# Channel sums by matmuls of 512 columns over four rows at a time, in three shifted banks, in place of one matmul of 384 columns for each row

## The chip, the cores and the metric

The kernel runs on one core of one Trainium2 chip. The metric is the device time of one execution in microseconds (us). The span in a profile starts and ends a little inside the measured time (532.4 us of span for a profiled run of 534.2 us), so spans are compared with spans and times with times.

## The reference

The input x is 384 x 384 pixels of 384 channels in bf16. Every channel is averaged over all pixels, the mean is scaled by one weight and passed through a sigmoid, and x is multiplied by that gate.

```python
g = jnp.einsum("bhwc->bc", x) / (H * W)      # H = W = C = 384, B = 1
s = gp[:, 0:C] * w1d[0]                      # k = 1: no padding, one tap
s = _sigmoid(s)
return x * s[:, None, None, :]
```

One property of these inputs matters for what the runs can prove. The weight is 0.00123 and no channel's mean is above 0.001 in size, so all 384 gates round to 0.5 in bf16. The output would be right with badly wrong sums, so "correct" says here that the data arrived and was multiplied, and does not prove the sums right.

## The kernel before

x is 147,456 rows of 384 channels: 1152 groups of 128 rows, one row for each partition. A "row" below is one such group: 384 elements, 768 bytes, on each of 128 partitions. Tiles of 45 and 44 rows are loaded into an arena that holds six of them. The first three tiles give an early gate; every tile is multiplied by that early gate and stored at once. The sums go on to the last tile only to check at the end that the early gate equals the true one in bf16. If it didn't, the whole pass would be run again.

```python
TILE = 45
AHEAD_TILES = 3
...
def add_rows(place, n, bank, first, last):          # TensorE: a sum over partitions and rows
    for i in range(n):
        plan.op("tensor",
            lambda e, i=i: e.matmul(acc[bank][:, :C], ones[:], at(place + i, 1),
                                    start=first and i == 0, stop=last and i == n - 1), ...)

def put(place, n, r0):                              # VectorE: the gate; ScalarE's queue: the store
    plan.op("vector", gate(place, n, s_early), reads=["s_early"] + rows(place, n), ...)
    plan.final.append(plan.dma("scalar", dram(o_rows, r0, n), at(place, n), ...))

for k, n in enumerate(sizes):
    place = ring.take(n)                            # an arena place: its old tile must be stored
    while inside and any(...): put(*inside.pop(0))
    load(place, n, r0)                              # SyncE's queue
    ...
    add_rows(place, n, 0 if k < AHEAD_TILES else 1, ...)     # condensed from two calls
    if k == AHEAD_TILES - 1:
        # VectorE: total <- acc[0]; ScalarE: s_early <- sigmoid(total * scale)
        ...
# after the last tile: total += acc[1], s_true, compare with s_early
```

The order of work for a tile is thus: load, sums (TensorE), gate (VectorE, which waits for the sums to have read the tile), store, and only then may a new load use the place.

## Time and profile before

| | before |
|---|---|
| time, median of the first 3 runs | 533.75 us (533.66 to 533.89) |
| bytes read and written | 113.25 + 113.25 MB |
| DMA rate in the steady state | 433 GB/s |
| TensorE busy | 243.2 us, 46% |
| VectorE busy | 236.7 us, 44% |
| blocks of instructions fetched | 9 |

First, lines from the page of the profile of the kernel before. The page's strips cut the span into 40 equal slices: the digits are tenths of busy time of TensorE (PE), VectorE (DVE) and the DMA engines, the next line is what they moved (a packet is counted whole in the slice where it starts, so single slices swing about the mean). "q8" is the queue that brings instructions: packets, MB, share of the DMA engines' time. The last two are groups of instructions: operation, shapes, count, then busy us and mean ns of one, then the idle time before them and what ended it.

```profile
...
PE   0979643347156156266266156266265255165100
...
DVE  0006999551642642633633642632633642633700
...
DMA  9999999999999999999999999999999999999995
GB/s 371 418 450 421 411 415 454 418 449 417 447 416 449 414 448 425 434 442 423 432 444 424 432 443 421 434 444 415 439 444 421 434 440 424 434 442 423 432 440 241
...
q8 instruction: 9, 0.15, 0.1%
...
L206 PE MATMUL acc<-arena,ones 128*128 128x384 bf16 x1152 | 243.0, 383 | 249.2 <-DMA arena<-in_x_dram 249.2
L165 DVE TENSOR_TENSOR arena<-arena,s_early 128x16896 bf16<-128x16896 bf16 (+1 forms) x26 | 234.1, 9019 | 224.3 <-PE acc L206 223.6
...
```

The DMA strip is full from the first slice to the last but one, while TensorE and VectorE are idle about half the time. Read this as: the DMA engines are the bound, and a busy or idle TensorE is a question for the waits. Next the windows view of the same kernel: for each stretch of time its length, the busy us of each engine with counts, TensorE's granted clock, the DMA's share and its rate in GB/s (by where a packet starts).

```profile
...
core 0: us, PE busy (x) PEld busy (x) DVE busy (x) ACT busy (x) POOL busy (x), PEclk, DMA share, GB/s
...
115.00:135.00 20.00, 9.72 (x45) 5.08 (x45) 8.67 (x2) 0.00 (x0) 0.00 (x0) 0.74 1.00 433
515.00:525.00 10.00, 0.00 (x0) 0.00 (x0) 0.00 (x0) 0.00 (x0) 0.00 (x0) 0.50 1.00 433
...
527.00:528.00 1.00, 0.00 (x0) 0.00 (x0) 0.00 (x0) 0.00 (x0) 0.00 (x0) 0.50 0.16 68
529.00:530.00 1.00, 0.00 (x0) 0.00 (x0) 0.00 (x0) 0.00 (x0) 0.00 (x0) 0.50 0.08 34
530.00:532.40 2.40, 0.00 (x0) 0.00 (x0) 0.00 (x0) 0.00 (x0) 0.00 (x0) 0.50 0.00 0
...
```

The rate is 433 GB/s both in the middle and ten microseconds before the end, when only stores are left. The Trainium skill ("DMA: Bandwidth & Descriptors", Specifications) gives 435 GB/s as the fabric ceiling for one core, and this trace agrees over long windows (single slices of the strip read up to 454, by the way in which packets are counted). Two short stretches will matter later: 68 GB/s at 527 to 528 us and 34 GB/s at 529 to 530 us.

The list of waits (engine, line and releaser: us in total, times, longest) and, after it, that of the queue which issues the loads:

```profile
...
PE acc L206 <- DMA arena<-in_x_dram: 249.2, 26, 18.0
DVE arena L165 <- PE acc L206: 223.6, 20, 11.9
...
```

```profile
...
SPq L99 <- DMA out_dram<-arena: 444.6, 20, 74.5
...
```

TensorE waits for loads, VectorE for TensorE, and the issue of loads waits for stores to free arena places. The waits for loads and stores are long while the DMA engines are full. That VectorE waits for TensorE doesn't show that a faster TensorE would help.

Finally the start, from the timeline of the same kernel (start, length, engine, line, operation): the sums of the third tile, the copy of the sums, the sigmoid, the first two gates and the issue of the first store.

```profile
...
35.46 9.07 PE L206 MATMUL acc<-arena,ones 128*128 128x384 bf16 x45 [3.95 <-DMA arena<-in_x_dram]
...
44.57 0.56 DVE L249 COPY total<-acc 128x384 f32<-128x384 f32 x1 [42.10 <-PE acc L206]
45.16 0.62 ACT L255 ACTIVATE s_early<-total,w_scaled 128x384 bf16<-128x384 f32 x1 [42.38 <-DVE total L249]
...
45.81 18.23 DVE L165 TENSOR_TENSOR arena<-arena,s_early 128x17280 bf16<-128x17280 bf16 x2 [0.68 <-ACT s_early L255]
55.00 0.38 ACTq L91 DMA_DIRECT2D out_dram<-arena  x1
...
```

The first store is issued at 55.00 us. Nothing can be stored before it, but six loads are in the queue and keep the DMA engines busy past 60 us.

### The profile page before, as it was taken

How to read it: one execution, taken by the hardware profiler on the slowest of the kernel's cores; microseconds unless marked ns; L12 is line 12 of the kernel's file. 1: busy time of each engine (PE TensorE's matmuls, PEld its weight loads, DVE VectorE, ACT ScalarE, POOL GpSimd, SP SyncE). 2: the span in 40 equal slices, each digit the busy share in tenths (PEclk: the TensorE clock that was granted, in tenths of full speed). 3: DMA queues.
4: the chain of work that ended last, by engine and by line, in shares of the span. 5: the costliest groups of instructions: out<-in, count | busy, mean ns of one | idle time of the engine just before them, and what ended most of it. 6: DMA issues, size and time to landing. Idle time of an engine off the chain costs nothing.

```text
span 532.4 us, 2500 instructions
## 1 busy us (share of the span) xinstructions
PE 243.2 (46%) x1153; PEld 127.8 (24%) x1153; DVE 236.7 (44%) x34; ACT 2.7 (1%) x4; POOL 0.3 (0%) x5
## 2 busy tenths in 40 slices
PE   0979643347156156266266156266265255165100
PEld 0435311123023033133133033033132133032000
DVE  0006999551642642633633642632633642633700
ACT  1000000000000000000000000000000000000000
POOL 0000000000000000000000000000000000000000
PEclk9989867587686786775676686786675686786755
DMA  9999999999999999999999999999999999999995
GB/s 371 418 450 421 411 415 454 418 449 417 447 416 449 414 448 425 434 442 423 432 444 424 432 443 421 434 444 415 439 444 421 434 440 424 434 442 423 432 440 241
DMA packets 7501, 226.66 MB, mean 426 GB/s; under 512 B 834, under 2 KB 834, under 8 KB 834
## 3 DMA queue, kind: packets, MB, share of 16 engines
q1 hardware_dynamic: 3744, 113.25, 49.6%
q10 hardware_dynamic: 3746, 113.25, 49.3%
q8 instruction: 9, 0.15, 0.1%
q14 instruction: 2, 0.02, 0.0%
HBM read 113.25 MB, written 113.25 MB: 425 GB/s over the span
## 4 chain that ended last, share of the span: by engine, by line
another core or an unknown queue 63%; DMA 20%; DVE 7%; PE 3%; SPq 1%; issue 1%; ACT 0%; DVEq 0%
DMA arena<-in_x_dram 12%; DMA out_dram<-arena 8%; DVE arena L165 7%; PE acc L206 3%; SPq L91 1%; ACT s_early L255 0%; ACT s_true L273 0%; DVE total L281 0%; DVE total L249 0%; DVE wrong L289 0%; DVE total L267 0%; SPq L99 0%; DVE redo L295 0%; DVEq L99 0%
## 5 line engine op out<-in xcount | busy, mean ns | idle before, releaser
L206 PE MATMUL acc<-arena,ones 128*128 128x384 bf16 x1152 | 243.0, 383 | 249.2 <-DMA arena<-in_x_dram 249.2
L165 DVE TENSOR_TENSOR arena<-arena,s_early 128x16896 bf16<-128x16896 bf16 (+1 forms) x26 | 234.1, 9019 | 224.3 <-PE acc L206 223.6
L206 PEld LDWEIGHTS acc<-arena,ones 128*128 128x128 bf16 x1152 | 127.7, 113 | 364.2 <-DMA arena<-in_x_dram 258.9
L249 DVE COPY total<-acc 128x384 f32<-128x384 f32 x1 | 0.6, 558 | 42.1 <-PE acc L206 42.1
L273 ACT ACTIVATE s_true<-total,w_scaled 128x384 bf16<-128x384 f32 x1 | 0.6, 615 | 458.2 <-DVE total L267 458.2
L177 ACT ACT_TABLE_LOAD x1 | 1.3, 1283 | 1.3 <-PEq L370 1.3
L183 PE MATMUL acc<-w_one,ones 1*128 1x1 bf16 x1 | 0.2, 158 | 2.0 <-DMA w_one<-in_w1d_dram 2.0
L281 DVE TENSOR_TENSOR total<-s_true,s_early 128x384 f32<-128x384 uint16 x1 | 0.6, 559 | 0.7 <-ACT s_true L273 0.7
L255 ACT ACTIVATE s_early<-total,w_scaled 128x384 bf16<-128x384 f32 x1 | 0.6, 616 | 42.4 <-DVE total L249 42.4
L192 DVE TENSOR_SCALAR w_scaled<-acc 128x1 f32<-128x1 f32 x2 | 0.2, 153 | 1.2 <-PE acc L183 1.2
L183 PEld LDWEIGHTS acc<-w_one,ones 1*128 1x128 bf16 x1 | 0.1, 99 | 2.0 <-issue 2.0
L289 DVE TENSOR_REDUCE wrong<-total 128x1 f32<-128x384 f32 x1 | 0.6, 553 | 0.0
L267 DVE TENSOR_TENSOR total<-total,acc 128x384 f32<-128x384 f32 x1 | 0.5, 546 | 0.0
L173 DVE MEMSET ones<- 128x128 bf16 x1 | 0.2, 165 | 0.8 <-PEq L370 0.8
L177 ACT ACTIVATE warm<-warm 128x1 f32<-128x1 f32 x1 | 0.2, 203 | 0.0
L295 DVE CAST redo<-wrong 128x1 int32<-128x1 f32 x1 | 0.2, 154 | 0.0
L370 POOL MEMSET const-bfloat16-1.0<- 128x1 bf16 x1 | 0.1, 102 | 0.0
L370 POOL MEMSET const-uint8-127<- 128x1 uint8 x1 | 0.1, 102 | 0.0
L172 POOL MEMSET warm<- 128x1 f32 x1 | 0.1, 99 | 0.3 <-POOLq L370 0.3
L370 POOL MEMSET const-float32-0.0<- 128x1 f32 x1 | 0.1, 99 | 0.2 <-issue 0.2
L370 POOL MEMSET const-float32-1.0<- 128x1 f32 x1 | 0.1, 99 | 0.0
## 6 DMA issues: line engine op xcount, KB each, us to landing
arena<-in_x_dram SPq DMA_DIRECT2D x18, 4224.0 KB, 28.9
out_dram<-arena ACTq DMA_DIRECT2D x18, 4224.0 KB, 72.2
arena<-in_x_dram SPq DMA_DIRECT2D x8, 4320.0 KB, 31.0
out_dram<-arena ACTq DMA_DIRECT2D x8, 4320.0 KB, 58.7
w_one<-in_w1d_dram ACTq DMA_DIRECT2D x1, 0.0 KB
```

What stands on the lines that cost most here:

```text
L91: ("op", lambda e: e.dma_start(out, in_), self.pool[i], 16)
L165: return lambda e: e.tensor_tensor(v, v, s_b, ALU.mult)
L177: lambda e: e.activation(warm[:, 1:2], warm[:, 0:1], ACT_F.Sigmoid),
L183: lambda e: e.matmul(acc[2][:, 0:1], ones[0:1, :], w_one[0:1, 0:1], start=True, stop=True),
L206: lambda e, i=i: e.matmul(acc[bank][:, :C], ones[:], at(place + i, 1), start=first and i == 0, stop=last and i == n - 1,),
L249: lambda e: e.tensor_copy(total[:], acc[0][:, :C]),
L255: lambda e: e.activation(s_early[:], total[:], ACT_F.Sigmoid, scale=w_scaled[:, 0:1]),
L267: lambda e: e.tensor_tensor(total[:], total[:], acc[1][:, :C], ALU.add),
L273: lambda e: e.activation(s_true[:], total[:], ACT_F.Sigmoid, scale=w_scaled[:, 1:2]),
L281: lambda e: e.tensor_tensor(total[:], s_true[:].bitcast(U16), s_early[:].bitcast(U16), ALU.not_equal),
L289: lambda e: e.reduce_max(wrong[:], total[:], axis=mybir.AxisListType.X),
L370: nc = _bacc.Bacc("TRN2", target_bir_lowering=False, num_devices=1)
```

## The change

The intent is to have fewer matmuls: four rows are 1536 contiguous columns, which three matmuls of 512 cover in place of four of 384. Since 512 is not a multiple of 384, matmul i starts at channel 128 x (i mod 3), so there are three banks with shifted channels, and VectorE joins them with six operations where there was one. Tiles have to be multiples of four rows, so they become 18 of 44 and 9 of 40 rows, 27 in place of 26. The diff, cut:

```diff
-TILE = 45
+TILE = 44
+WIDE = 512
...
-    acc = [nc.alloc_psum_tensor(f"acc{i}", [P, 512], F32) for i in range(3)]
+    acc = [[nc.alloc_psum_tensor(f"acc{g}_{i}", [P, WIDE], F32) for i in range(3)]
+           for g in range(2)]
...
-    sizes = split(n_rows, TILE)
+    sizes = [4 * q for q in split(n_rows // 4, TILE // 4)]
...
-    def add_rows(place, n, bank, first, last):
-        for i in range(n):
+    def add_rows(place, n, group, first, last):
+        n_wide = n * C // WIDE
+        start = place * C
+        for i in range(n_wide):
+            bank = acc[group][i % 3]
...
-                lambda e, i=i: e.matmul(acc[bank][:, :C], ones[:], at(place + i, 1), ...),
+                lambda e, i=i, bank=bank: e.matmul(bank[:, :], ones[:],
+                    arena[:, start + i * WIDE : start + (i + 1) * WIDE],
+                    start=first and i < 3, stop=last and i >= n_wide - 3),
...
+    def add_banks(group, copy):
+        for m, lo, hi in ((0, 0, C), (0, C, WIDE), (1, 0, 256), (1, 256, WIDE),
+                          (2, 0, P), (2, P, WIDE)):
+            c = (128 * m + lo) % C
+            part = total[:, c : c + hi - lo]
+            of = acc[group][m][:, lo:hi]
+            # the first one copies where copy is set, the others add
...
-            plan.op("vector", lambda e: e.tensor_copy(total[:], acc[0][:, :C]), ...)
+            add_banks(0, copy=True)
...
-    plan.op("vector", lambda e: e.tensor_tensor(total[:], total[:], acc[1][:, :C], ALU.add), ...)
+    add_banks(1, copy=False)
```

More of the change, by code (lines that the diff above doesn't have):

```diff
@@ L134, in bass_standalone__channel_attn_eca__vision_kernel @@
     B, H, W, C = x.shape
-    assert B == 1 and C == ROW and (B * H * W) % P == 0
+    assert B == 1 and C == ROW and (B * H * W) % (4 * P) == 0
     n_rows = B * H * W // P
@@ L152, in bass_standalone__channel_attn_eca__vision_kernel @@
     arena = nc.alloc_sbuf_tensor("arena", [P, n_arena * C], BF16)
-    acc = [nc.alloc_psum_tensor(f"acc{i}", [P, 512], F32) for i in range(3)]
+    acc = [
+        [nc.alloc_psum_tensor(f"acc{g}_{i}", [P, WIDE], F32) for i in range(3)]
+        for g in range(2)
+    ]
+    w_all = nc.alloc_psum_tensor("w_all", [P, WIDE], F32)
     def at(r0, n):
@@ L183, in bass_standalone__channel_attn_eca__vision_kernel @@
         lambda e: e.matmul(
-            acc[2][:, 0:1], ones[0:1, :], w_one[0:1, 0:1], start=True, stop=True
+            w_all[:, 0:1], ones[0:1, :], w_one[0:1, 0:1], start=True, stop=True
         ),
         reads=["ones", "w_one"],
-        writes=["acc2"],
+        writes=["w_all"],
     )
@@ L192, in bass_standalone__channel_attn_eca__vision_kernel @@
             lambda e, i=i, n=n: e.tensor_scalar_mul(
-                w_scaled[:, i : i + 1], acc[2][:, 0:1], 1.0 / float(P * n)
+                w_scaled[:, i : i + 1], w_all[:, 0:1], 1.0 / float(P * n)
             ),
-            reads=["acc2"],
+            reads=["w_all"],
             writes=[f"w_scaled{i}"],
@@ L200, in load @@
         plan.dma("sync", at(place, n), dram(x_rows, r0, n), writes=rows(place, n))
-    def add_rows(place, n, bank, first, last):
-        for i in range(n):
+    def add_rows(place, n, group, first, last):
[3 more added lines that the diff above has]
+            bank = acc[group][i % 3]
             plan.op(
                 "tensor",
-                lambda e, i=i: e.matmul(
-                    acc[bank][:, :C],
+                lambda e, i=i, bank=bank: e.matmul(
+                    bank[:, :],
                     ones[:],
-                    at(place + i, 1),
-                    start=first and i == 0,
-                    stop=last and i == n - 1,
-                ),
-                reads=["ones"] + (rows(place, n) if i in (0, n - 1) else []),
-                writes=[f"acc{bank}"],
-                signal=i == n - 1,
-            )
+                    arena[:, start + i * WIDE : start + (i + 1) * WIDE],
+                    start=first and i < 3,
+                    stop=last and i >= n_wide - 3,
+                ),
+                reads=["ones"] + (rows(place, n) if i in (0, n_wide - 1) else []),
+                writes=[f"acc{group}"],
+                signal=i == n_wide - 1,
+            )
+    def add_banks(group, copy):
[4 more added lines that the diff above has]
+            of = acc[group][m][:, lo:hi]
+            if copy and (m, lo) == (0, 0):
+                emit = lambda e, part=part, of=of: e.tensor_copy(part, of)
+            else:
+                emit = lambda e, part=part, of=of: e.tensor_tensor(
+                    part, part, of, ALU.add
+                )
+            plan.op("vector", emit, reads=[f"acc{group}", "total"], writes=["total"])
     def put(place, n, r0):
@@ L246, in bass_standalone__channel_attn_eca__vision_kernel @@
         if k == AHEAD_TILES - 1:
-            plan.op(
-                "vector",
-                lambda e: e.tensor_copy(total[:], acc[0][:, :C]),
-                reads=["acc0"],
-                writes=["total"],
-            )
+            add_banks(0, copy=True)
             plan.op(
@@ L262, in bass_standalone__channel_attn_eca__vision_kernel @@
         put(*tile)
-    plan.op(
-        "vector",
-        lambda e: e.tensor_tensor(total[:], total[:], acc[1][:, :C], ALU.add),
-        reads=["total", "acc1"],
-        writes=["total"],
-    )
+    add_banks(1, copy=False)
     plan.op(
```

## The prediction

> **What bounds the kernel now.** It moves 226.5 MB, and the DMA engines are full nearly throughout: the page's 40-slice strip has 9 in every DMA slice but the last. By windows: 361 GB/s in 0 to 13.8 us (start-up), then 429 to 442 nearly everywhere (416 and 408 where stores begin), 433 in the steady 20 us cycles of one tile in and one out, still 433 at 515 to 525 us, nothing after about 527; the rest to 532.4 us is the program's end. The Trainium skill ("DMA: Bandwidth & Descriptors", Specifications) gives 435 GB/s as the fabric ceiling; the measured 433 agrees. So the time is bytes over one rate, plus about 2 us of start and 5.5 us of end.
>
> TensorE is busy 46%, VectorE 44% of the span; in the wait list TensorE waits 249 us for loads, VectorE 224 us for TensorE, and SyncE 445 us for stores to free arena space.
>
> **What the change does.**
> - TensorE: 1152 matmuls of 384 columns become 864 of 512: the same 442,368 columns. Warm, a burst of 45 took 7.49 us, 166 ns each; cold, they were 320 ns apart. The skill ("TensorE: Matmul & The Clock Gate", Back-to-back issue gap) has N/2.4 + 2.5 ns warm and N/1.2 cold: only the small fixed part shrinks. Estimate: bursts of 44 rows, 8.8 to 10.3 us, get 1 to 2% shorter; busy 243 to about 239 us. Weight loads fall to 864, but they overlap.
> - VectorE: one copy (558 ns, 384 columns) and one add (546 ns) become six operations each, 1536 columns. From 153 ns for one column and 550 for 384 I estimate 6 x 0.15 + 1536 x 1.03 ns = 2.5 us, 2.6 with gaps: +2.1 us, twice.
> - Tiles: 26 (8 of 45, 18 of 44 rows) become 27 (18 of 44, 9 of 40). Six tiles fit in the arena before and after. One load and one store are added in full queues; bytes are unchanged.
>
> **Critical path.** Before, the third tile lands at 35.5 us, TensorE takes 9.1, copy and sigmoid 1.3, the gate 9.2, and the first store is issued at 55.0. Now: landing 34.7, sums 8.9, adds 2.6, sigmoid 0.65, gate 9.0: about 55.9, +0.9 us. But six loads are queued, 26 MB, lasting alone to about 63 us, so the DMA does not starve. At the end the last store was issued at 503.5, with 23 us of queue still to drain, its own 10 us included; the final adds come after the last gate, and the check ends near 508 instead of 506, far before 527. Neither saving nor adds lie on the bounding path. I expect no visible gain.
>
> **Prediction:** 534.0 us, range 531.8 to 537.0. Chances: faster by over 2% 0.01, within 2% 0.96, slower by over 2% 0.03.
>
> **What would show it right.** Steady windows near 433 GB/s, DMA strip full; 864 matmuls near 427 ns apart cold and 218 warm; two trains of six adds, 2.6 us each; first store near 56 us; TensorE and VectorE idle as long or longer; last bytes near 527 us. Wrong if the DMA shows a gap at 55 to 65 us, or the queue drains before the last store is issued.
>
> **What would make it wrong.** Rows of 30,720 bytes per partition (40-row tiles) moving at another rate than 33,792 and 34,560 (both ran at 432 to 433); loads and stores interleaving differently after the shift of sizes; a failed early check, which would rerun the whole pass and nearly double the time (gates from 132 rows instead of 135, so very unlikely).

## The result

The changed kernel took 532.85 us (median of 6 runs, 532.57 to 534.44) against 533.81 us for the kernel before (6 runs, 533.46 to 535.01). The ratio is 0.9983 with a 95% interval of 0.9968 to 0.9999, which is within 2%. Here and below a ratio is the mean time of one kernel's fast runs over that of the other's in the same rounds, so it is not quite the ratio of the medians quoted beside it. The forecast was 534.0 us; the kernel came out 0.9 us faster than before where 0.25 us slower was forecast.

The same lines of the page for the changed kernel (the wide matmuls are listed once for each bank):

```profile
...
PE   0877560527516516427437426425625632662300
...
DVE  0007999462463362461461562464164256326620
...
DMA  8999999999999999999999999999999999999996
GB/s 367 443 419 440 407 438 417 447 425 430 443 428 433 436 425 440 435 420 445 436 420 440 433 428 426 440 444 428 429 434 432 427 437 437 421 437 440 423 438 280
...
q8 instruction: 7, 0.11, 0.1%
...
L170 DVE TENSOR_TENSOR arena<-arena,s_early 128x16896 bf16<-128x16896 bf16 (+1 forms) x27 | 234.2, 8691 | 224.8 <-PE acc_2 L215 224.1
L215 PE MATMUL acc_0<-arena,ones 128*128 128x512 bf16 x282 | 127.5, 452 | 236.1 <-DMA arena<-in_x_dram 235.6
L215 PE MATMUL acc_1<-arena,ones 128*128 128x512 bf16 x283 | 125.6, 444 | 19.9 <-DMA arena<-in_x_dram 19.5
L215 PE MATMUL acc_2<-arena,ones 128*128 128x512 bf16 x282 | 124.1, 440 | 0.8 <-issue 0.7
...
```

The DMA strip is as full as before. The columns are the same, so TensorE's busy time hardly moves: 237.0 us on the page. The three groups hold 282 + 283 + 282 = 847 of the 864 wide matmuls; the others are missing from the records. Two later traces of kernels with the same 864 matmuls have all of them, with 241.0 and 241.8 us, so what was saved is about 2 us; the granted clock moves this figure too (a later trace of the same matmuls has 246.7 us with 847 of them recorded). What did fall is the number of instruction blocks, from 9 to 7.

The windows of the changed kernel, in the same columns:

```profile
...
115.00:135.00 20.00, 10.21 (x32) 3.90 (x33) 8.60 (x2) 0.00 (x0) 0.00 (x0) 0.67 1.00 433
515.00:525.00 10.00, 0.00 (x0) 0.00 (x0) 0.00 (x0) 0.00 (x0) 0.00 (x0) 0.50 0.98 421
...
527.00:528.00 1.00, 0.00 (x0) 0.00 (x0) 0.00 (x0) 0.00 (x0) 0.00 (x0) 0.50 0.08 31
529.00:530.00 1.00, 0.00 (x0) 0.00 (x0) 0.00 (x0) 0.00 (x0) 0.00 (x0) 0.50 0.00 0
530.00:532.40 2.40, 0.00 (x0) 0.00 (x0) 0.00 (x0) 0.00 (x0) 0.00 (x0) 0.50 0.01 3
...
```

The rate in the middle is 433 GB/s in both. The small bursts at the end differ: 31 GB/s at 527 to 528 us and nothing after it but the end of the program. The last piece of data came earlier.

The waits, and those of the loads' queue, have hardly moved (TensorE's wait for loads fell from 249.2 to 235.6 us):

```profile
...
PE acc_0 L215 <- DMA arena<-in_x_dram: 235.6, 26, 11.7
DVE arena L170 <- PE acc_2 L215: 224.1, 21, 11.8
...
```

```profile
...
SPq L99 <- DMA out_dram<-arena: 449.7, 21, 71.2
...
```

The start in the timeline of the changed kernel: the copy, five adds (shown in groups), the sigmoid, the first two gates and the issue of the first store.

```profile
...
42.24 0.56 DVE L235 COPY total<-acc_0 128x384 f32<-128x384 f32 x1 [39.77 <-remote]
42.83 0.29 DVE L237 TENSOR_TENSOR total<-total,acc_0 128x128 f32<-128x128 f32 x1
43.15 0.87 DVE L237 TENSOR_TENSOR total<-total,acc_1 128x256 f32<-128x256 f32 x2
44.06 0.87 DVE L237 TENSOR_TENSOR total<-total,acc_2 128x128 f32<-128x128 f32 x2
...
44.97 0.61 ACT L274 ACTIVATE s_early<-total,w_scaled 128x384 bf16<-128x384 f32 x1 [42.18 <-DVE total L237]
...
45.62 17.83 DVE L170 TENSOR_TENSOR arena<-arena,s_early 128x16896 bf16<-128x16896 bf16 x2 [0.68 <-ACT s_early L274]
...
54.61 0.38 ACTq L91 DMA_DIRECT2D out_dram<-arena  x1
...
```

The six operations take from 42.24 to 44.93 us, 2.7 us in place of 0.6. The first store is nevertheless issued at 54.61 us, 0.4 us earlier than before. The experiments explain the first of the small surprises, the earlier start, and the second, the earlier end, only in part.

### The profile page after: what moved, and what is told of

Read it like the earlier page. It is cut to its first block, busy times and chain, and to the rows that moved or that the text cites. A ratio compares the mean times of both kernels' runs of the same rounds, so it can differ in the third digit from the quotient of the medians.

```text
span 531.1 us, 1925 instructions
## 1 busy us (share of the span) xinstructions
PE 237.0 (45%) x848; PEld 94.2 (18%) x865; DVE 240.8 (45%) x45; ACT 2.7 (1%) x4; POOL 0.3 (0%) x5
## 4 chain that ended last, share of the span: by engine, by line
another core or an unknown queue 72%; DMA 13%; DVE 7%; PE 2%; SPq 1%; issue 1%; ACT 0%; DVEq 0%
DMA out_dram<-arena 7%; DVE arena L170 6%; DMA arena<-in_x_dram 5%; SPq L91 1%; DVE total L237 1%; PE acc_0 L215 1%; PE acc_1 L215 0%; PE acc_2 L215 0%; DMA w_one<-in_w1d_dram 0%; ACT s_true L287 0%; ACT s_early L274 0%; DVE total L295 0%; DVE total L235 0%; DVE wrong L303 0%
## 5 line engine op out<-in xcount | busy, mean ns | idle before, releaser
L215 PE MATMUL acc_0<-arena,ones 128*128 128x512 bf16 x282 | 127.5, 452 | 236.1 <-DMA arena<-in_x_dram 235.6
L215 PE MATMUL acc_1<-arena,ones 128*128 128x512 bf16 x283 | 125.6, 444 | 19.9 <-DMA arena<-in_x_dram 19.5
L215 PE MATMUL acc_2<-arena,ones 128*128 128x512 bf16 x282 | 124.1, 440 | 0.8 <-issue 0.7
L215 PEld LDWEIGHTS acc_0<-arena,ones 128*128 128x128 bf16 x288 | 32.1, 111 | 309.9 <-DMA arena<-in_x_dram 267.3
L215 PEld LDWEIGHTS acc_2<-arena,ones 128*128 128x128 bf16 x288 | 32.3, 112 | 47.4 <-issue 23.6
L215 PEld LDWEIGHTS acc_1<-arena,ones 128*128 128x128 bf16 x288 | 32.1, 112 | 41.6 <-issue 18.9
L237 DVE TENSOR_TENSOR total<-total,acc_2 128x128 f32<-128x128 f32 (+1 forms) x4 | 1.7, 420 | 0.1
L237 DVE TENSOR_TENSOR total<-total,acc_1 128x256 f32<-128x256 f32 x4 | 1.7, 420 | 0.1
L237 DVE TENSOR_TENSOR total<-total,acc_0 128x128 f32<-128x128 f32 (+1 forms) x3 | 1.1, 374 | 0.1
L274 ACT ACTIVATE s_early<-total,w_scaled 128x384 bf16<-128x384 f32 x1 | 0.6, 615 | 42.2 <-DVE total L237 42.2
```

Of the source, the lines that this page charges most:

```text
L215: lambda e, i=i, bank=bank: e.matmul(bank[:, :], ones[:], arena[:, start + i * WIDE : start + (i + 1) * WIDE], start=first and i < 3, stop ...
L237: emit = lambda e, part=part, of=of: e.tensor_tensor(part, part, of, ALU.add)
L274: lambda e: e.activation(s_early[:], total[:], ACT_F.Sigmoid, scale=w_scaled[:, 0:1]),
```

## The experiments

Theory A was that of the prediction: only the bytes on the DMA engines count. After the two traces two rivals were formed. Theory B: what was gained comes from fewer TensorE instructions, because instructions come through the same DMA engines as the data. Theory C: the length of the sums counts after all.

Theory B rests on the landings in the trace. A transfer is split over the 16 DMA engines and each reports its own end. The following numbers are worked out from those records (us from the span's start); they are not lines of a view.

```
third load,  before:   15 engines end at 33.52 to 34.23, one at 35.41   (instruction block at 32.2)
third load,  changed:  16 engines end at 32.72 to 33.32                 (no block yet)
fourth load, changed:  15 engines end at 42.74 to 43.34, one at 44.41   (instruction block at 38.6)
last store,  before:   first engine 526.39, last engine 530.69, spread 4.30;  span 532.4
last store,  changed:  first engine 526.37, last engine 529.35, spread 2.98;  span 531.1
```

In both kernels one engine falls 1.1 to 1.2 us behind the others in the load that is moving while the first block of instructions is fetched. The block itself took 1.07 us. The traces of the runs below agree: in all twelve traces whose first block comes during the first five loads, one engine and no other falls behind in the load that is moving, by 0.9 to 1.8 us. The changed kernel with weights held, whose first block comes at 76 us, has no engine behind in those loads. In the run with each matmul in three parts, the blocks at 23.0, 33.2, 42.2 and 52.4 us leave one, two, three and four engines behind. So a block holds up one engine, and these four held up four different ones.

At the end the first engine is done at the same time in both kernels; the last two differ, the very last by 1.3 us, which is the whole difference of the spans (532.4 - 531.1). Some of it is this one execution: the profiled run of the kernel before was 0.45 us above its median, that of the changed kernel 0.09. In all fourteen traces the program ended 1.71 to 1.73 us after the last landing. So the question is what the last of the 16 engines had to do beyond the others.

The Trainium skill ("Runtime: NRT & Kernel Launch", Instruction fetch mechanics) says that instructions are fetched in blocks of 16 KiB, 256 instructions. The traces agree to within a block: a matmul with its weight load is two instructions; 1153 of them make 2306, which is 9.0 blocks, and 9 blocks of 16,384 bytes were fetched; the 865 of the changed kernel make 6.8 blocks, and 7 were fetched. The same section calls the cost of crossing into a new block "mostly hidden". The first group of experiments measures that.

### Old sums on the new tiles

```diff
 # on the kernel before
-    sizes = split(n_rows, TILE)
+    sizes = [4 * q for q in split(n_rows // 4, 11)]
```

> The tiles of the changed kernel (18 of 44, 9 of 40 rows) with the old 384-wide sums, one copy and one add. Theory A (only the DMA bytes count; sums and adds lie off the bounding path, and what little was gained comes from the tile sizes): as the changed kernel, 532.9 us. Theory B (the small gain comes from fewer TensorE instructions: the trace shows 9 blocks of 16 KB of instructions fetched before and 7 after, which share the DMA engines with the data and delay the one that ends last): back at 533.8 us, with 9 blocks, and the 16 landings of the last store spread over 4.3 us as before, not 3.0. Theory C (the length of the sums counts): 533.8 us or more.

It took 533.15 us (533.05 to 533.64, 5 runs) against 533.71 us for the kernel before in the same rounds; ratio 0.9991, interval 0.9978 to 1.0005. Nine blocks were fetched and the spread was 3.37 us. This lies between the theories: the median is 0.3 us above the changed kernel's and 0.6 us below the old one's. Neither step is resolved by the interval, so this run alone decides nothing.

### No sums after the third tile

```diff
 # on the kernel before
-        else:
-            add_rows(place, n, 1, k == AHEAD_TILES, k == len(sizes) - 1)
...
 # the last add is dropped, and s_true is made from the early sums
```

> The kernel before without the sums of tiles 4 to 26 (the final check then compares the early gates with themselves; the output is still right). TensorE work falls from 1152 to 135 matmuls, and gates no longer wait for it. A: 533.8 us within 0.5. B: 1 or 2 instruction blocks in place of 9, at about 0.65 us each (1.3 us of spread for two blocks): about 529 us. C: faster by many us, since each tile's store no longer waits 9 to 10 us for its sums.

It took 531.82 us (531.59 to 532.36); ratio 0.9967, interval 0.9953 to 0.9980. The line of the instruction queue on its page:

```profile
...
q8 instruction: 1, 0.02, 0.0%
...
```

Theory C falls for the steady state: TensorE's busy time went from 243 to 27 us, and the kernel gained 1.9 us. Theory A, which allowed 0.5 us, falls as well. Theory B has the right sign, but its 0.65 us a block is too much: 8 blocks fewer gave 1.9 us. The spread was 1.70 us.

### Each matmul in three parts

```diff
 # on the kernel before: all but the first row of a group and the last row of a tile
-        for i in range(n):
-            ... matmul(acc[bank][:, :C], ones, row i)
+        for i in range(n):
+            whole = (first and i == 0) or i == n - 1
+            for c, w in [(0, C)] if whole else [(0, P), (P, P), (2 * P, P)]:
+                ... matmul(acc[bank][:, c : c + w], ones, row i [c : c + w])
```

> The kernel before with nearly every 384-wide matmul cut into three of 128 columns: the same columns, but about 3,300 matmuls and 26 blocks of instructions in place of 9. A: the 17 added blocks are 0.28 MB, 0.6 us at 433 GB/s: 534.4 us. B: 17 blocks at 0.65 us on the engine that ends last: about 545 us. C: sums of a tile take perhaps 10 to 14 us in place of 9 to 10: some us slower.

It took 538.09 us (537.45 to 538.61); ratio 1.0083, interval 1.0069 to 1.0097. TensorE's columns are the same and its busy time is 246 us, but:

```profile
...
q8 instruction: 26, 0.43, 0.3%
...
```

The first engine was done at 526.25 us, as always, and the last at 533.94: a spread of 7.69 us. So 17 more blocks cost 4.4 us (538.09 - 533.71), 0.26 us a block. As plain bytes at 433 GB/s they would cost 0.64 us in all (17 x 16,384 bytes); if all of them fell on the engine that ends last, at a sixteenth of that rate, about 10 us. Theory B holds in kind and its size had to be corrected. Blocks and instructions rise together in these runs, so the times alone can't tell the cost of a block from another cost of each instruction; what ties it to the blocks are the landings above, where each block is followed by one more engine that is late.

### Weights loaded once for each tile

The ones are the weights of every matmul, yet each matmul loads them again. Here only the first matmul of a tile does.

```diff
 # on the changed kernel; held_matmul emits the matmul without its weight load
-                lambda e, i=i, bank=bank: e.matmul(
+                lambda e, i=i, bank=bank: (
+                    e.matmul if i == 0 else lambda *m, **k: held_matmul(e, *m, **k)
+                )(
```

> The changed kernel with the ones loaded into the array once for each tile in place of once for each matmul: 864 matmuls but 27 weight loads, so about 900 TensorE instructions, 3 or 4 blocks in place of 7. Columns, adds and tiles are those of the changed kernel. A: 532.9 us. B: 3 to 4 blocks less, at 0.65 us: about 530.7 us. C: sums as long as before (the loads overlap): 532.9 us.

It took 532.40 us (531.96 to 532.62); ratio to the kernel before 0.9974, interval 0.9960 to 0.9987. Three blocks were fetched, the spread was 1.92 us, and the busy line of the page reads:

```profile
...
PE 241.7 (46%) x865; PEld 2.9 (1%) x28; DVE 240.8 (45%) x45; ACT 2.7 (1%) x4; POOL 0.3 (0%) x5
...
```

837 weight loads fewer leave TensorE's busy time where it was (241.0 us in another trace of the same matmuls that loads the ones each time): the loads did overlap, and what they cost was their fetching. The gain, 0.45 us for four blocks against the changed kernel's 532.85 of other rounds, is small: the 530.7 us of theory B failed, and it is also only half of what a quarter of a microsecond a block would give.

The same edit on the kernel before, with 4 blocks on the old tiles:

```diff
-                lambda e, i=i: e.matmul(
+                lambda e, i=i: (
+                    e.matmul if i == 0 else lambda *m, **k: held_matmul(e, *m, **k)
+                )(
```

> The kernel before with the ones loaded once for each tile: 1152 matmuls and 27 loads, about 1180 TensorE instructions, 4 blocks in place of 9, on the old tiles of 45 and 44 rows. With the slope of the first four runs (24 times 16 KB more moved the spread of the last landings by 6.0 us, 0.25 us a block): 533.7 - 5 x 0.25 = 532.5 us, spread about 3 us in place of 4.3. If the tiles alone made the gain of the change: 533.7 us.

It took 532.85 us (532.40 to 534.66, 6 runs) against 533.75; ratio 0.9988, interval 0.9976 to 1.0000. The spread was 3.10 us. This lies between the two expectations, nearer to that of the blocks. So the old tiles and the old 384 columns reach the changed kernel's median time without its three banks and six adds.

This run also tests the earlier start. The tiles are the old ones, and the first block comes at 48.6 us in place of 32.2: the third load landed at 34.28 us in place of 35.41, and the first store was issued at 53.97 in place of 55.00. The reverse case is the run with old sums on the new tiles: its first block came at 31.3 us, in the third load, and the last piece of that load landed at 34.49 us, 1.2 us later than in the changed kernel with the same tiles.

All of these together, with the landings of the last store from one trace each:

| kernel | tiles | blocks | first landing | last landing | spread | time, median |
|---|---|---|---|---|---|---|
| no late sums | old | 1 | 526.49 | 528.19 | 1.70 | 531.82 |
| before, weights held | old | 4 | 526.22 | 529.33 | 3.10 | 532.85 |
| before | old | 9 | 526.39 | 530.69 | 4.30 | 533.7 to 533.8 |
| thirds | old | 26 | 526.25 | 533.94 | 7.69 | 538.09 |
| changed, weights held | new | 3 | 526.54 | 528.46 | 1.92 | 532.40 |
| changed | new | 7 | 526.37 | 529.35 | 2.98 | 532.85 |
| changed, three trains of adds (below) | new | 7 | 526.43 | 529.79 | 3.36 | 533.00 |
| narrow sums on new tiles | new | 9 | 526.17 | 529.55 | 3.37 | 533.15 |
| doubled sums, held (below; a stall at the start) | old | 9 | 534.21 | 537.67 | 3.46 | 541.67 |
| changed, nine trains of adds (below; a stall at the start) | new | 7 | 540.41 | 545.30 | 4.89 | 548.31 |

In the runs without a stall the first landing stays within 0.4 us. Over the wide range the last landing follows the blocks: 6.0 us of spread for 25 blocks on the old tiles, 0.24 us a block. Over a few blocks it does not: the three traces with 7 blocks on the new tiles have spreads of 2.98, 3.36 and 4.89 us, and the two with 9 blocks on the old tiles 4.30 and 3.46 us. Traces with the same count thus differ by 0.8 to 1.9 us, about as much as the whole gain of the change, and the count alone does not set the end.

The medians are steadier. Taken between kernels on the same tiles, they give 0.11 us a block (changed, with and without held weights), 0.15 (narrow and wide sums on the new tiles, which differ in the adds too), 0.18 (before, with and without held weights) and 0.26 (thirds). So of the 0.96 us that separates the medians, an estimated 0.2 to 0.5 us goes with the 2 blocks fewer, and the rest goes with the tiles or with chance: the narrow sums on new tiles, with the same 9 blocks, were 0.6 us faster than the kernel before, in runs whose interval includes no difference. Why tiles of 44 and 40 rows should end closer together was not found out. One difference is the piece of the last store: 33,792 bytes, which took 1.25 us, before, and 30,720 bytes and 1.14 us after; no run separates it. The records do not name the engine of a packet either, so how the later blocks are dealt out among the engines, and how their delays add up by the end, is open.

### More adds at the start

The next runs ask why 2.1 us more on VectorE in the chain to the first store cost nothing. The train of six operations is repeated; each train begins with the copy, so the result stands.

```diff
 # on the changed kernel
-            add_banks(0, copy=True)
+            for _ in range(3):          # the second run has 9
+                add_banks(0, copy=True)
```

> The changed kernel with the early train of six bank adds run three times (each begins with a copy, so the result stands): VectorE is delayed by 5.4 us more, the first store goes out near 60 us in place of 54.6, before the six loads in the queue are drained (62 to 64 us). If the adds are off the bounding path with some 8 us of slack: 532.9 us within 0.7. If they are on it: about 538.3 us.

> The same with nine trains: 21.8 us more, the first store near 76.4 us. The queue of loads is empty from about 63 us, so the slack of 8 us or so is used up and the rest shows: 544 to 548 us, with a hole in the DMA strip between 63 and 77 us. If VectorE had no part in it at all: 532.9 us.

Three trains: 533.00 us (532.47 to 533.29); the first store was issued at 59.95 us in place of 54.61, and the time moved by 0.15 us. Nine trains: 548.31 us (548.05 to 550.16), ratio 1.0279, interval 1.0266 to 1.0292; the first store was issued at 74.91 us; 544 to 548 us had been expected. The windows of the run with nine trains (the same columns as before; the last number is GB/s):

```profile
...
60.00:62.00 2.00, 1.84 (x9) 0.64 (x7) 1.83 (x6) 0.00 (x0) 0.00 (x0) 1.00 0.99 422
62.00:64.00 2.00, 0.00 (x0) 0.00 (x0) 1.86 (x5) 0.00 (x0) 0.00 (x0) 1.00 0.04 17
64.00:74.00 10.00, 7.30 (x33) 3.15 (x33) 9.25 (x4) 0.61 (x1) 0.00 (x0) 1.00 0.00 1
74.00:76.00 2.00, 0.00 (x0) 0.00 (x0) 2.00 (x2) 0.00 (x0) 0.00 (x0) 1.00 0.63 270
...
```

At about 63 us the six loads are done and no store is there yet: the DMA engines move next to nothing for 12 us, in a kernel that is otherwise bound by them. The first store came 20.3 us later than in the changed kernel and the time grew by 15.5 us. The landings divide this: the last store's first landing came 14.0 us later (540.41 against 526.37), and the rest is its wider spread (4.89 us, with the same 7 blocks). So about 6.3 us of delay are free, and the edge lies near 60.9 us (54.61 + 6.3); the first store at 59.95 us, with three trains, is inside it. The edge is 2 us earlier than the end of the six loads; 0.87 us of that is the time from the issue of the store to its first packet. The expectation for four tiles, further below, was written with a rougher edge, 59.4 us, which takes all of the 15.5 us for the stall.

### Doubled sums

```diff
 # on the kernel before, with the weights held as above
-        for i in range(n):
+        for j in range(2 * n):
+            i = j // 2                  # each row is added twice, the scale is halved
```

> The kernel before (384 wide, 45 and 44 rows) with every matmul issued twice into the same sum (the mean divided by two), and the ones loaded once for each tile: 2304 matmuls and 26 loads, so again 9 blocks of instructions, but sums of a tile last about 16 to 18 us in place of 9 to 10. If only bytes and blocks count: 533.7 us within 0.7. If the length of the sums lies on the bounding path: about 7 us or more slower at the start and the end, 540 us or more.

It took 541.67 us (541.17 to 542.08); ratio 1.0150, interval 1.0137 to 1.0163. My first reading, that only bytes and blocks count, missed this by 8 us. The other expectation, 540 us or more if the length of the sums lies on the bounding path, was met. Blocks are the same 9, and the spread of the last store was 3.46 us. The windows show where the time went:

```profile
...
62.00:64.00 2.00, 2.00 (x14) 0.00 (x0) 2.00 (x1) 0.00 (x0) 0.00 (x0) 1.00 0.69 294
64.00:70.00 6.00, 6.00 (x39) 0.00 (x0) 6.00 (x2) 0.00 (x0) 0.00 (x0) 1.00 0.01 6
70.00:72.00 2.00, 2.00 (x14) 0.00 (x0) 2.00 (x1) 0.00 (x0) 0.00 (x0) 1.00 0.64 276
...
```

The doubled sums of the first three tiles run one after the other and delay the first store to 70.02 us. From 64 to 70 us the DMA engines start next to nothing. The hole is there once, at the start: from 96 to 115 us the rate is 435 GB/s, and the windows from 480 to 530 us have 426 to 436, with TensorE busy 77% of the span. So the length of the sums is off the bounding path for the same reason as the adds, the queue of loads, and only up to such an edge.

### An arena of four tiles

```diff
 # on the changed kernel, and again with three trains of adds
-    n_arena = nc.sbuf_bytes_remaining // (2 * C)
+    n_arena = 4 * TILE                  # 176 rows
```

> The changed kernel with an arena of 4 tiles (176 rows) in place of 6. The run with nine trains issued its first store at 74.9 us and lost 15.5 us, so stores issued by about 59.4 us cost nothing with six tiles queued; with four, the queue of loads is drained two tiles (20.1 us) earlier and that point moves to about 39.3 us. The first store at 54.6 us is then 15.3 us late: about 548.2 us. If the start did not matter and only the steady state did: 532.9 us.

> The same with the early adds run three times: 5.4 us more on VectorE, which cost nothing with six tiles in the arena (533.0 against 532.9 us). With four tiles nothing hides them: 5.4 us over the run with four tiles and one train, about 553.6 us. If the adds stay hidden: the same as that run.

With one train it took 550.03 us (549.18 to 550.49); ratio 1.0303, interval 1.0289 to 1.0317. With three it took 555.86 us (554.14 to 556.73). The DMA strip of the run with one train, and then its windows around the hole:

```profile
...
DMA  9991999999999999999999999999999999999966
...
```

```profile
...
42.00:44.00 2.00, 0.00 (x0) 0.00 (x0) 1.25 (x4) 0.61 (x1) 0.00 (x0) 1.00 0.04 17
44.00:52.00 8.00, 7.22 (x26) 2.99 (x27) 8.00 (x1) 0.00 (x0) 0.00 (x0) 0.79 0.00 0
52.00:54.00 2.00, 1.76 (x9) 0.59 (x6) 2.00 (x2) 0.00 (x0) 0.00 (x0) 1.00 0.63 270
...
```

Four loads are done at about 43 us, and nothing moves until the first store at 52.80 us. The direction and most of the size were foreseen (548.2 us). The rest of the 17.2 us lies at the end: the last two slices of the strip are at 6, because with four places the stores of earlier tiles run out while the last tile is still being gated: the store before the last had landed at 531.5 us, and the last gate ended at 534.6. With six places that did not happen. The spread of the last store is another finding here: 0.58 us, with the same 7 blocks. The queues had run dry before it, so all engines began it level. The same shows after the stall with nine trains, where the next load landed within 0.17 us on all engines: a delay of one engine is lost when the queues run dry. The two trains more, which were worth 0.15 us with six places, now cost 5.8 us; 5.4 had been expected.

The same arena with the old sums on the new tiles:

```diff
 # on the kernel with old sums on the new tiles
-    n_arena = nc.sbuf_bytes_remaining // (2 * C)
+    n_arena = 176
```

> The tiles of the changed kernel with the old sums, one copy and one add, and the same arena of four tiles. Its first store is issued at 53.7 us, 0.9 us before the changed kernel's (2.1 us of adds less, sums a little longer), and nothing hides that any more, against 0.3 to 0.5 us for two more blocks of instructions: about 0.5 us faster than the changed kernel with four tiles, so the change would there be a small loss in place of a small gain.

It took 550.53 us (549.84 to 551.70), not faster than the changed kernel's 550.03; the intervals of the two ratios (1.0302 to 1.0330 and 1.0289 to 1.0317) overlap. This expectation failed. Its premise was a first store 0.9 us earlier than the changed kernel's; in the traces it was 53.70 us against 52.80. In that trace of the changed kernel TensorE kept the full granted clock from 17.6 to 44.9 us, while in its trace with six places the clock fell to half from 33.1 to 36.5 us, during the third tile's sums; those sums ended at 40.4 us in place of 42.2. Such a difference of clock is as large as the adds themselves, so this pair can't say whether the change would gain or lose where nothing hides it.

### A try for a better version

```diff
 # on the changed kernel with weights held
-TILE = 44
+TILE = 24
```

> A try for a better version: the wide sums with the ones loaded once for each tile, and 48 tiles of 24 rows (11 in the arena). About 910 TensorE instructions, 3 or 4 blocks; smaller pieces should end closer together. If smaller tiles narrow the spread of the last landings below 1.9 us: about 531.8 us. If twice as many transfers cost anything on full queues: 532.4 us or more.

It took 534.49 us (534.22 to 534.63); ratio 1.0013, interval 1.0000 to 1.0027. Three blocks, a spread of 2.38 us, but all engines ended late: the first landing of the last store was at 528.32 us in place of 526.2 to 526.5. The windows between 100 and 500 us gave 431 to 432 GB/s where the changed kernel has 432 to 433. Some 42 more transfers on full queues do cost something, about 2 us in all (528.3 - 526.4); whether by the count of transfers or by the shorter rows was not separated. The best version remains the changed kernel with weights held: 532.40 us, 1.3 us or 0.26% below the kernel before and 0.45 us below the changed one.

## Why the prediction was right

- *The DMA engines bound the kernel, at 433 GB/s.* Right: the strip is full in both profiles, and the run without late sums, in which TensorE's work fell by nine tenths, gained only 1.9 us.
- *The sums only shrink by their small fixed part.* Right, and less than said. The changed matmuls follow each other at 0.215 us warm (17.04, 17.25, 17.47 us) and 0.43 us cold, as the Trainium skill has it ("TensorE: Matmul & The Clock Gate", Wait — 56ns, not 53.3ns?: 215.7 ns warm and 426.7 ns cold measured for 512 columns). The section that the prediction names, Back-to-back issue gap, gives its formula for an isolated matmul, and about 131 ns a matmul for a stream of weight loads and matmuls of 512 columns; this case is such a stream, and its trace does not agree with the 131 ns. Busy time went from 243 to 241 us where every record is there, not to 239.
- *Six operations in place of one, 2.6 us.* Right: 2.7 us.
- *The first store 0.9 us later, at 55.9 us.* Wrong: it was 0.4 us earlier, at 54.61 us. The term that failed is the landing of the third tile, put at 34.7 us and measured at 33.3 us. In the kernel before one engine had delivered its part of that tile 1.2 us after the others, with an instruction block fetched during that load. The changed kernel fetches its first block later, at 38.6 in place of 32.2 us. The two runs that shift the first block, described above, show the same.
- *Six loads hide it all; the queue lasts to about 63 us.* Right, and tested from both sides: up to about 61 us the first store is free, and past that every microsecond counts. With four places the adds cost their full time. This slack is also why the wrong first store did the forecast no harm.
- *Bytes over one rate, plus fixed ends of 2 and 5.5 us; no visible gain.* Right within the range, wrong in its sign: +0.25 us was forecast and -0.96 us measured. The term that was mis-sized is the end. It isn't fixed: it is 1.72 us plus the spread of the 16 engines at the last store, 4.30 us before and 2.98 us after in one trace each. The prediction read the bytes as ending near 527 us, while the same trace has 68 GB/s at 527 to 528 us and a last piece at 529 to 530. The prediction noted that weight loads fall to 864 and that they overlap; that they must be fetched, by the bounding engines, was not counted. By the slopes above that is 0.2 to 0.5 us of the gain; the rest is not settled.

## What to carry to other kernels

In a kernel bound by its DMA engines, as this one is, a saving on TensorE or VectorE was worth nothing, and a cost was free, as long as the transfers in the queue lasted; so work out when they run dry before counting either. Instructions are data too: the first blocks of 16 KB held up one engine each here, and fewer blocks (weights loaded once for a run of matmuls) gained 0.1 to 0.2 us a block, while cutting matmuls into parts cost 0.26. This kernel ended with its slowest engine, so look at how far apart the engines land before calling an end a constant; and take more than one trace, since two with the same blocks differed by up to 1.9 us.

## What the Trainium skill lacked or had wrong

- "Runtime: NRT & Kernel Launch", Instruction fetch mechanics, calls the fetch of a further block mostly hidden. In this kernel, with DMA engines that are always full, 25 blocks more widened the last store's landings from 1.70 to 7.69 us and took the time from 531.82 to 538.09 us, about 0.25 us a block (runs that differ by 2 to 5 blocks gave 0.11 to 0.18), and the first block left one engine 0.9 to 1.8 us late in the load that was moving.
- "DMA: Bandwidth & Descriptors", Specifications, lists about 358 GB/s as the HBM limit for a core and doesn't say there when it holds; further down, under Measured, the page gives 425 GB/s for a core whose neighbour is idle, so it does not lack this. With one core running, the kernel before held 432 to 434 GB/s from 100 to 500 us (reads and writes together) and 425 GB/s over the whole span.
- "DMA: Bandwidth & Descriptors" says that the engines of a transfer finish independently, but gives no size. Here the 16 landings of the last store lay 1.7 to 7.7 us apart on full queues and 0.6 to 1.1 us where the queues had run dry before it, and the program's end followed the last of them by 1.71 to 1.73 us in all fourteen traces.
